# Local attention and a feed-forward net on one core: the first batch's values loaded once, by channels, and the instruction order written anew

## The chip, the core and the metric

The kernel runs on one core of a Trainium2 chip, in one launch. The metric is the device time of a launch in microseconds; with one core there is one time for each run.

## What is computed

For each of 4 batches and 8 heads, 768 queries of 64 channels attend to the keys within 15 positions of their own and, besides, to 24 block keys (the maximum of k over each block of 32 positions), whose values are the block means of v. The heads' results, side by side, are the 512 channels of 3072 tokens, which pass through a gated net of width 2048.

```python
k_sum = k.reshape(B, H, nb, block, D).max(axis=3)
v_sum = v.reshape(B, H, nb, block, D).mean(axis=3)
mask_l = np.abs(pos[:, None] - pos[None, :]) < window
scores_all = np.concatenate([np.where(mask_l, scale * q @ k.T, -1e9), scale * q @ k_sum.T + np.log(block)], axis=-1)
out = softmax(scores_all) @ np.concatenate([v, v_sum], axis=2)
x = out.transpose(0, 2, 1, 3).reshape(B * S, H * D)
h = x @ w_in
y = (h / (1 + np.exp(-h))) @ w_out
```

## The kernel before

The work is cut into 24 attention stages of 128 tokens (six of a batch) and 12 chunks of 256 tokens for the net. Stage s has scores (`scores`, L706), a softmax that DVE and ACT share (`job_a`: L731 subtracts and finds the maximum, L735 is the exponential), turned probabilities (L744 for the first four stages) and the product with the values (`job_c`, L776), after which `job_x` scales the result into the chunk's input. Chunk c and one eighth f of the net's width give a first product FFN1 (`job_f`, L997 in full float32 for the first chunk, L1005 with split float16 operands), a gate and a second product FFN2 (L1014). From the fifth chunk on, chunks go in pairs with seven products in place of eight (`pair_f`, L1082, L1133, L1204).

The sixteen weight tiles come as 64-bit words, 1 MB each, and are unpacked on chip: ACT (L913), POOL or DVE (L909, L911) and DVE (L915), which takes 1.2 us for each. Until its weight comes, the home of a weight (`wr`, named `wt` in the rows) holds data of the first batch: `staging` hands such homes out, and the load of that weight waits until the data in them has been read.

Values of the first batch come twice. `job_mean` loads them by tokens (`v0`, six tiles of 128 x 512, L624); TensorE multiplies each by a matrix `blocks` with 1/32 in the right places and so sums the block means in one bank (L628), DVE takes each tile's largest magnitude (L631). The means are copied from the bank five times (L265 on ACT, L269 on DVE): to the value tiles of stages 0 and 1, and to `vms`, from which `side_v` sends them to the value tiles of stages 2 and 3 by DMA. Those value tiles' other 96 rows, tokens of the two half stages, come from `v` by `main_v` (L603). The maximum over the six columns goes through a small matmul (`v_scale`, L513), whose result scales the first batch's values.

What engine does what, and in which order, is in no loop. Every step is a `plan.op` with the engines that can do it and what it reads and writes. The table `ORDER` (three characters a step) lists all steps in order with an engine for each, and `replay` takes it as it is when its length fits. Each engine runs its own list in that order, waiting where a step's inputs are not there. `replay` also fills holes that it foresees on PE at the start with matmuls on the identity (L386). SP issues nearly all DMAs, in order: a load whose destination is still in use holds back those behind it.

Of the kernel before, what the change touches and what calls it, by code (L numbers as in the profile page):

```python
# [9 lines left out]
F32 = mybir.dt.float32  # L10
# [5 lines left out]
ALU = mybir.AluOpType  # L16
# [242 lines left out]
def local_attn_ffn(ctx: ExitStack, tc: tile.TileContext, q0, qkT, qF, qkD, kF, v0, v, vR, w, out):  # L259
# [56 lines left out]
    blocks = const.tile([P, HWIN + 11 * 4], F32, name="blocks")  # L316
# [44 lines left out]
    vm_t = const.tile([P, 4, NB], F32, name="vm")  # L361
# [206 lines left out]
    def job_qk(s, prio):  # L568
        prio += nudge("qk", s)
        b, t = divmod(s, NTILE)  # L570
        if s < NPL:
            qk = qk_t[s % 2].bitcast(F32)[:, :4 * P].rearrange("p (a n) -> p a n", a=4)
            for hp in range(0, 4, 2):
                first = s == 0 and hp == 0
                plan.op({"dma": 545}, lambda e, hp=hp, first=first: (nc.scalar if first else nc.sync).dma_start(out=qk[:, hp:hp + 2], in_=q0[t, :, hp:hp + 2]), w=[("qk", s % 2, hp + i) for i in range(2)], prio=prio + hp // 2, cols=1 if first else 0)
            return
# [37 lines left out]
    def job_mean(prio):  # L614
        prio += nudge("mean")
        k = sbank()
        for t in range(NTILE):
            at = (NTILE - 1 - t) * 4
            if t < NPL:
                main_v(t, prio + 5)  # L620
            stg, key = staging(-1)
            src, cost = stg[:, :DM], 603
            parts = [(src, blocks[:, at:at + NKEY])]
            plan.op({"dma": 755}, lambda e, src=src, t=t: nc.sync.dma_start(out=src, in_=v0[t]), w=key, prio=prio)  # L624

# [12 lines left out]
        v_scale(0, prio)  # L638
# [252 lines left out]
    def job_w(fp, kind, prio):  # L891
# [7 lines left out]
        if wide:  # L899
            rt = home.rearrange("p (c i) -> p c i", i=2)  # L900
            low, top = rt[:, :, 0], rt[:, :, 1]
            sides = [k + x for k in mine for x in ((0,), (1,), (0, "side"), (1, "side"))]
# [515 lines left out]
NUDGE = {}  # L1418


_INS = ["q0", "qkT", "qF", "qkD", "kF", "v0", "v", "vR", "w"]


def _layout(inputs):
# [55 lines left out]
```

## Time and profile before

| | |
|---|---|
| median of 3 runs | 571.44 us (570.43 to 573.02) |
| profiled execution | 569.17 us, span 567.2 us |
| PE, DVE, ACT, POOL busy | 556.8, 467.8, 404.8, 210.8 us |
| DMA | 79.88 MB, 141 GB/s over the span |
| first float32 FFN1 matmul | 26.3 us after the span's start |
| last PE matmul ends | 563.1 us after the span's start |

Engines: PE is TensorE's matmul, DVE VectorE, ACT ScalarE, POOL GpSimd, SP the engine that issues DMAs. A busy PE is not PE at its peak, since matmuls overlap and their ends are modelled. Times within the span count from its first instruction. The column of the granted clock reads 1.00 in every stretch of this run.

### The profile page before, as it was taken

What the parts mean: (1) busy time and instruction counts of PE and PEld (TensorE: products, weight loads), DVE (VectorE), ACT (ScalarE), POOL (GpSimd) and SP (SyncE); (2) the same over time, 40 slices, a digit from 0 to 9 for tenths busy, and PEclk for the clock granted to TensorE, in tenths of its full rate; (3) what the DMA queues carried; (4) which work ended last, traced back from release to release, by engine and by line L of the source; (5) the groups of instructions that cost most, each with busy time, mean ns of one, the idle gap of its engine ahead of it and who ended that gap; (6) DMA issues with size and microseconds to landing.
All of it is one profiled execution on the core that took longest, in us unless ns stands there. A gap on an engine that the chain in (4) does not pass through costs nothing.

```text
span 567.2 us, 15166 instructions
## 1 busy us (share of the span) xinstructions
PE 556.8 (98%) x5811; PEld 392.0 (69%) x5811; DVE 467.8 (82%) x1245; ACT 404.8 (71%) x977; POOL 210.8 (37%) x261
## 2 busy tenths in 40 slices
PE   9899999999999999999999999999999999999997
PEld 5677666667676767767766656676666766688886
DVE  6898899999899888888687867866566698899996
ACT  4799999978878986766586866765755586477531
POOL 2052533253333641234724250346642453143310
PEclk9999999999999999999999999999999999999999
DMA  9969955486667672373525594454363212100002
GB/s 327 340 237 362 397 193 159 112 204 171 166 122 154 203 164 69 103 189 91 174 47 142 154 212 129 122 153 83 128 148 81 64 40 47 67 1 2 1 1 74
DMA packets 65351, 79.88 MB, mean 141 GB/s; under 512 B 46304, under 2 KB 48352, under 8 KB 63232
## 3 DMA queue, kind: packets, MB, share of 16 engines
q1 hardware_dynamic: 65136, 78.80, 49.0%
q8 instruction: 45, 0.74, 0.6%
q14 instruction: 26, 0.21, 0.2%
q10 hardware_dynamic: 144, 0.13, 0.1%
HBM read 59.97 MB, written 6.29 MB: 117 GB/s over the span
## 4 chain that ended last, share of the span: by engine, by line
PE 85%; DVE 6%; DMA 3%; ACT 3%; issue 1%; POOL 1%; SPq 1%; DVEq 0%; ACTq 0%; POOLq 0%
PE bank L1133 19%; PE bank L1082 19%; PE bank L1014 16%; PE bank L1005 13%; PE bank L1204 6%; PE bank L706 3%; PE bank L794 3%; PE bank L997 3%; DVE wt L1173 1%; PE bank L386 1%; DMA raw<-in_qkD_dram 1%; DVE t L1157 1%; DMA raw<-in_qF_dram 1%; DMA raw<-in_kF_dram 1%; ACT e L735 1%
## 5 line engine op out<-in xcount | busy, mean ns | idle before, releaser
L1082 PE MATMUL bank<-wt 128*128 128x256 f16 x1248 | 152.7, 273 | 1.5 <-DVE t L1062 0.9
L1082 PEld LDWEIGHTS <-wt 128*128 128x128 f16 x1248 | 121.1, 98 | 31.7 <-issue 2.6
L1014 PE MATMUL bank<-wt,g 128*128 128x512 f16 (+1 forms) x352 | 97.3, 420 | 0.0
L735 ACT ACTIVATE e<-e,mx 128x120 f32<-128x120 f32 x192 | 73.4, 384 | 19.9 <-DVE mx L731 19.7
L1005 PE MATMUL bank<-xh,wt 128*128 128x256 f16 x448 | 80.8, 273 | 0.0
L1005 PEld LDWEIGHTS <-wt 128*128 128x128 f16 x672 | 65.0, 98 | 16.1 <-issue 3.4
L1133 PE MATMUL bank<-wt,g 128*128 128x512 f16 x288 | 69.9, 380 | 0.1
L1005 PE MATMUL bank<-xl,wt 128*128 128x256 f16 x224 | 61.1, 273 | 0.0
L1061 ACT ACTIVATE t<-bank,asc 128x512 f32<-128x512 f32 x48 | 32.2, 682 | 27.0 <-PE bank L1082 23.8
L1014 PEld LDWEIGHTS <-g 128*128 128x128 f16 x288 | 27.9, 98 | 27.9 <-ACT t L1022 0.2
L1133 PE MATMUL bank<-wt,xl 128*128 128x512 f16 x192 | 46.1, 380 | 0.0
L731 DVE CUSTOM_DVE_ANT_0 e<-bank,masks,qsc 128x120 f32<-128x120 f32 x144 | 42.7, 337 | 3.9 <-PE bank L706 2.1
L1133 PEld LDWEIGHTS <-g 128*128 128x128 f16 x288 | 27.7, 98 | 25.2 <-POOL g L283 0.6
L1062 DVE SCALAR_TENSOR_TENSOR t<-t,bank 128x512 f32<-128x512 f32 x48 | 32.4, 684 | 14.0 <-ACT t L1061 13.5
L275 POOL TENSOR_SCALAR e<-e,sum 128x120 f32<-128x120 f32 x49 | 21.1, 437 | 53.9 <-DVE sum L750 49.8
L735 ACT ACTIVATION_READ_ACCUMULATOR e<-e,mx 128x1 f32 x192 | 36.1, 188 | 0.0
L283 POOL TENSOR_TENSOR g<-t,g 128x512 f16<-128x512 f32 x21 | 24.3, 1157 | 30.6 <-PE bank L794 7.4
L1133 PEld LDWEIGHTS <-xl 128*128 128x128 f16 x192 | 18.7, 98 | 17.5
L1022 ACT ACTIVATE t<-bank,asc 128x512 f32<-128x512 f32 x28 | 19.1, 683 | 13.3 <-PE bank L1005 13.2
L283 POOL TENSOR_TENSOR p<-e,p 128x480 f16<-128x480 f32 x19 | 20.8, 1096 | 20.6 <-ACT p L265 8.2
L265 ACT CAST g<-t 128x512 f16<-128x512 f32 x41 | 25.1, 612 | 4.2 <-DVE t L1024 2.3
L1108 DVE TENSOR_TENSOR bank<-bank,xh 128x256 f32<-128x256 f32 x32 | 13.8, 430 | 14.9 <-PE bank L1082 10.9
(266 smaller groups left out, 1187.3 us busy)
## 6 DMA issues: line engine op xcount, KB each, us to landing
wt<-in_w_dram SPq DMA_DIRECT2D x16, 1024.0 KB
raw<-in_qkD_dram SPq DMA_DIRECT2D x18, 624.0 KB
raw<-in_v_dram SPq DMA_DIRECT2D x20, 512.0 KB
out_dram<-raw SPq DMA_DIRECT2D x20, 256.0 KB
raw<-in_kF_dram SPq DMA_DIRECT2D x12, 384.0 KB
raw<-in_qF_dram SPq DMA_DIRECT2D x9, 512.0 KB
raw<-in_vR_dram SPq DMA_DIRECT2D x12, 384.0 KB
raw<-vms SPq DMA_DIRECT2D x40, 48.0 KB
```

The source lines that it names most:

```text
L265: nc.scalar.copy(out=out, in_=in_)
L275: nc.gpsimd.tensor_scalar(out=out, in0=in_, scalar1=by, scalar2=0.0, op0=ALU.mult, op1=ALU.add)
L283: eng[e].tensor_tensor(out=out, in0=in0, in1=in1, op=ALU.subtract)
L731: plan.op({"dve": 195 if b == 0 else 255}, lambda e, k=k, at=at, et=et, mx=mx: nc.vector.tensor_tensor_reduce(out=et, in0=bank[k][:, at:at ...
L735: plan.op({"act": 375}, lambda e, et=et, mx=mx, total=total: nc.scalar.activation(out=et, in_=et, func=AF.Exp, scale=-1.0, bias=mx, accum_ ...
L1005: nc.tensor.matmul(out=h[:, d * CH:(d + 1) * CH], lhsT=wt[f, 0][:, part, d, ct * P:(ct + 1) * P], rhs=x[:, ct, :], start=(ct == 0 and q == ...
L1014: nc.tensor.matmul(out=bank[to][:, :z0 - a0], lhsT=a[:, d * CH + u * P:d * CH + u * P + P], rhs=b[:, d, a0:z0], start=(opens and d == 0 an ...
L1061: plan.op({"act": 586}, lambda e: nc.scalar.activation(out=t, in_=h, func=AF.Tanh, scale=asc_t[c // 3 % 2][:, f:f + 1]), r=[("bank", k), ( ...
L1062: plan.op({"dve": 605}, lambda e: nc.vector.scalar_tensor_tensor(out=t, in0=t, scalar=1.0, in1=h, op0=ALU.add, op1=ALU.mult), r=[("bank", ...
L1082: nc.tensor.matmul(out=to, lhsT=w2[part][:, ct * P:(ct + 1) * P], rhs=xs[j][:, x, ct, :], start=(opens and ct == 0 and q == 0), stop=(ct = ...
L1133: nc.tensor.matmul(out=bank[to], lhsT=a[:, d * CH + v * P:d * CH + v * P + P], rhs=wt[f, 1][:, b][:, d, :], start=(opens and d == 0 and q ...
L1204: nc.tensor.matmul(out=place(m), lhsT=a[pa], rhs=b[pb], start=(opens and not right and q == 0), stop=(closes and q == 2), skip_group_check ...
```

## The change

The first batch's values now come by channels (`vR`, four tiles of 128 x 768, as the later batches' do). DVE sums each over blocks of 32 (L628 of the new kernel) and takes its largest magnitude (L630). TensorE turns the value rows of stages 0 and 1 out of these tiles (four groups of four transposes, L643, into banks 6 and 7) and the block sums (four transposes, L651, into bank 1, after GpSimd has put zeros ahead of the sums so that they land in rows 96 to 119). ACT and DVE copy them home, four copies of 96 rows and five of 24 rows, each of these with the factor 1/32 and all with the channels put back in order. `v0`, `blocks` and the six matmuls are gone, and so are two of the four loads of `main_v`. The queries of stages 1 to 3 come in one load each instead of two. `ORDER` is a new table for the whole kernel. In all, 35 filling matmuls become 62, and the other instructions of PE are the same in number save those named.

```diff
-    nc.vector.memset(blocks, 0.0)
-    for j in range(4):
-        nc.vector.memset(blocks[j * BLK:(j + 1) * BLK, HWIN + 20 + j:HWIN + 21 + j], 1.0 / BLK)
...
-    vm_t = const.tile([P, 4, NB], F32, name="vm")
+    vmp_t = const.tile([P, 4, NKEY], F32, name="vm")
+    vm_t = vmp_t[:, :, HWIN:]
+    nc.gpsimd.memset(vmp_t[:, :, :HWIN], 0.0)
...
-            for hp in range(0, 4, 2):
+            step = 4 if s else 2
+            for hp in range(0, 4, step):
...
     def main_v(t, prio):
         stg, key = staging(0)
         plain_v[t] = stg[:, :2 * DM].rearrange("p (a c) -> p a c", a=2), [key[0], key[0] + ("side",), key[0] + ("side", 1)]
-        plan.op({"dma": 1700}, lambda e: nc.sync.dma_start(out=plain_v[t][0][:HWIN], in_=v[0, t, :HWIN]), w=key, prio=prio)
+        if t < 2:
+            plain_v[t][1].insert(1, key[0] + ("u", 1))
+            return
+        plan.op({"dma": 1850}, lambda e: nc.sync.dma_start(out=plain_v[t][0][:HWIN], in_=v[0, t, :HWIN]), w=key, prio=prio)
...
     def job_mean(prio):
         prio += nudge("mean")
-        k = sbank()
-        for t in range(NTILE):
-            at = (NTILE - 1 - t) * 4
-            if t < NPL:
-                main_v(t, prio + 5)
+        for t in range(NPL):
+            main_v(t, prio + 5)
+        vrs, vkeys = [], []
+        for j in range(4):
             stg, key = staging(-1)
-            src, cost = stg[:, :DM], 603
-            parts = [(src, blocks[:, at:at + NKEY])]
-            plan.op({"dma": 755}, lambda e, src=src, t=t: nc.sync.dma_start(out=src, in_=v0[t]), w=key, prio=prio)
-
-            def mean(e, parts=parts, t=t):
-                for n, (rows, of) in enumerate(parts):
-                    nc.tensor.matmul(out=bank[k][:NKEY], lhsT=of, rhs=rows, start=(t == 0 and n == 0), stop=(t == NTILE - 1))
-
-            plan.op({"pe": 970}, mean, r=key, w=[("bank", k)], prio=prio, cols=2048)
-            plan.op({"dve": cost}, lambda e, src=src, t=t: nc.vector.tensor_reduce(out=am_t[:src.shape[0], t:t + 1], in_=src, axis=AX.X, op=ALU.max, apply_absolute_value=True), r=key, w=[("am", t)], prio=prio, port=())
+            nc.vector.memset(stg[:, :HALO], 0.0)
+            vr = stg[:, HALO:HALO + S]
+            vrs.append(stg)
+            vkeys += key
+            plan.op({"dma": 1250}, lambda e, vr=vr, j=j: nc.sync.dma_start(out=vr, in_=vR[0, :, j, :]), w=key, prio=prio)
+            plan.op({"dve": 869}, lambda e, vr=vr, j=j: nc.vector.tensor_reduce(out=vm_t[:, j, :], in_=vr.rearrange("p (n k) -> p n k", k=BLK), axis=AX.X, op=ALU.add),
+                    r=key, w=[("vm", j)], prio=prio, port=())
+            plan.op({"dve": 869}, lambda e, vr=vr, j=j: nc.vector.tensor_reduce(out=am_t[:, j:j + 1], in_=vr, axis=AX.X, op=ALU.max, apply_absolute_value=True), r=key, w=[("am", j)], prio=prio, port=())
+        def order(t):
+            return t.rearrange("n (h r q) -> n r h q", h=H, r=4)
+
+        def turned(k, rows):
+            return bank[k][rows].rearrange("n (r h q) -> n r h q", r=4, h=H)
+
         for t in range(2):
             for u in range(2):
-                to, key = plain_v[t][0][HWIN:NKEY, u], plain_v[t][1][1 + u:2 + u]
-                plan.op({"act": 478, "dve": 598}, lambda e, k=k, to=to: copy(e, to, bank[k][HWIN:NKEY]), r=[("bank", k)], w=key, prio=prio, port=())
-        plan.op({"act": 478, "dve": 598}, lambda e, k=k: copy(e, vms_t[HWIN:NKEY], bank[k][HWIN:NKEY]), r=[("bank", k)], w=["vms"], prio=prio, port=())
-        am_sum(NTILE, prio)
+                k, at = (6, 7)[u], t * P + u * HALF
+
+                def part(e, k=k, at=at):
+                    for j in range(4):
+                        nc.tensor.transpose(out=bank[k][:HWIN, j * P:(j + 1) * P], in_=vrs[j][:, at:at + HWIN], identity=ident)
+
+                to, key = plain_v[t][0][:HWIN, u], plain_v[t][1][u:u + 1]
+                plan.op({"pe": 520}, part, r=vkeys, w=[("bank", k)], prio=prio, cols=512)
+                plan.op({"act": 605, "dve": 605}, lambda e, k=k, to=to: copy(e, order(to), turned(k, slice(0, HWIN))), r=[("bank", k)], w=key, prio=prio, port=())
+
+        def turn_sums(e):
+            for j in range(4):
+                nc.tensor.transpose(out=bank[1][:NKEY, j * P:(j + 1) * P], in_=vmp_t[:, j, :], identity=ident)
+
+        plan.op({"pe": 520}, turn_sums, r=[("vm", j) for j in range(4)], w=[("bank", 1)], prio=prio, cols=512)
+        low = slice(HWIN, NKEY)
+        homes = [(plain_v[t][0][low, u], plain_v[t][1][2 + u:3 + u]) for t in range(2) for u in range(2)] + [(vms_t[low], ["vms"])]
+        for to, key in homes:
+            plan.op({"act": 605, "dve": 605}, lambda e, to=to: times(e, order(to), turned(1, low), 1.0 / BLK), r=[("bank", 1)], w=key, prio=prio, port=())
+        am_sum(4, prio)
         v_scale(0, prio)
...
-_INS = ["q0", "qkT", "qF", "qkD", "kF", "v0", "v", "vR", "w"]
+_INS = ["q0", "qkT", "qF", "qkD", "kF", "v", "vR", "w"]
```

The order moves at three places. DVE, from the copies of the turned values to the second half of `xp`, the input of the first FFN1; before (`bank_181` holds the block means, `bank_182` the stage's attention product, L915 is the weight's unpacking):

```order
L269 COPY vms<-bank_181 24x512
L269 COPY wt<-bank_181 24x512
L816 RECIPROCAL ss_150<-ss_150 128x8
L818 CAST sh_152<-ss_150 128x8
L269 COPY wt<-bank_179 120x512
L819 TENSOR_TENSOR sh_152<-ss_150,sh_152 128x8
L832 TENSOR_TENSOR xp<-bank_182,xr_154 128x4x128
L516 TENSOR_REDUCE sc_139<-bank_181 128x1
L517 TENSOR_SCALAR sc_139<-sc_139 128x1
L518 TENSOR_SCALAR sc_139<-sc_139 128x1
L915 SCALAR_TENSOR_TENSOR wt<-wt 128x1024
L832 TENSOR_TENSOR xp<-bank_182,xr_155 128x4x128
```

and after (`bank_176` and `bank_177` hold turned values or, for L853, the product; L936 is the unpacking):

```order
L269 COPY wt<-bank_174 120x512
L269 COPY wt<-bank_176 96x4x8x16
L836 TENSOR_SCALAR ss_145<-ss_145 128x8
L837 RECIPROCAL ss_145<-ss_145 128x8
L839 CAST sh_147<-ss_145 128x8
L840 TENSOR_TENSOR sh_147<-ss_145,sh_147 128x8
L853 TENSOR_TENSOR xp<-bank_177,xr_149 128x4x128
L936 SCALAR_TENSOR_TENSOR wt<-wt 128x1024
L346 COPY masks<-masks 128x120 x2
L347 MEMSET masks 64x15
L348 MEMSET masks 64x17
L853 TENSOR_TENSOR xp<-bank_177,xr_150 128x4x128
```

Two of the five small copies of means stood here before; now turned values and probabilities do, the maximum over the partition sums (L516 to L518) has gone behind, and the edges of the masks (L346 to L348) have come ahead.

DVE behind the second half of `xp`, after (before, four rows of L631 stood ahead of it instead, and behind it came L731, L911 and L915):

```order
L936 SCALAR_TENSOR_TENSOR wt<-wt 128x1024
L958 TENSOR_SCALAR wm<-wm 128x1
L630 TENSOR_REDUCE am<-wt 128x1 x2
L752 ISA e,mx<-bank_174,band 128x120
L752 ISA mx 128x1
L630 TENSOR_REDUCE am<-wt 128x1
L936 SCALAR_TENSOR_TENSOR wt<-wt 128x1024
L504 TENSOR_REDUCE am<-am 128x1
L1045 SCALAR_TENSOR_TENSOR g_167<-t_165,bank_170 128x512
L269 COPY wt<-bank_175 120x512
L836 TENSOR_SCALAR ss_144<-ss_144 128x8
L514 TENSOR_REDUCE sc_134<-bank_176 128x1
```

The four reductions for the largest magnitude (L630, one more at row 72, just behind `xp`) now stand between the softmax of stage 2 and the unpackings L936, ahead of the first gated product L1045.

SP's loads of the weights; before (`wt_64` and on are the homes of the weights, even numbers of the first product; `wt_68` to `wt_71` held `v0`):

```order
L903 DMA wt_64<-in_w_dram 128x2048
L603 DMA wt_76<-in_v_dram 96x1024
L575 DMA qk0_128<-in_q0_dram 128x256
L603 DMA wt_77<-in_v_dram 96x1024
L575 DMA qk0_128<-in_q0_dram 128x256
L903 DMA wt_66<-in_w_dram 128x2048
L903 DMA wt_65<-in_w_dram 128x2048
L903 DMA wt_68<-in_w_dram 128x2048
L903 DMA wt_70<-in_w_dram 128x2048
L575 DMA qk1_129<-in_q0_dram 128x256 x2
L903 DMA wt_67<-in_w_dram 128x2048
L603 DMA wt_76<-in_v_dram 96x1024
```

and after (`wt_68` to `wt_71` hold `vR`):

```order
L924 DMA wt_64<-in_w_dram 128x2048
L924 DMA wt_65<-in_w_dram 128x2048
L924 DMA wt_66<-in_w_dram 128x2048
L924 DMA wt_67<-in_w_dram 128x2048
L612 DMA wt_76<-vms_133 24x512 x2
L574 DMA qk1_123<-in_q0_dram 128x512
L924 DMA wt_70<-in_w_dram 128x2048
L605 DMA wt_76<-in_v_dram 96x1024
L924 DMA wt_68<-in_w_dram 128x2048
L924 DMA wt_69<-in_w_dram 128x2048
L671 DMA raw2_121<-in_v_dram 128x1024
L924 DMA wt_72<-in_w_dram 128x2048
```

The first four weights now follow each other, and the weights in `wt_70`, `wt_68`, `wt_69` (in this order) come behind the `vms` copies and the last queries.

## Rows read from the trace of the kernel before

**Rows 1.** The profile's page, part 1: busy time, share of the span, instructions of each engine.

```profile
PE 556.8 (98%) x5811; PEld 392.0 (69%) x5811; DVE 467.8 (82%) x1245; ACT 404.8 (71%) x977; POOL 210.8 (37%) x261
```

**Rows 2.** Waits of PE from 28 us on: line, whom it waited for: us in total, times, longest.

```profile
PE bank L1082 <- DVE t L1062: 0.9, 2, 0.8
PE bank L706 <- DVE wt L280: 0.5, 1, 0.5
PE bank L706 <- DVE qk L595: 0.5, 2, 0.3
```

**Rows 3.** The chain that ended last, 0 to 70 us, in order: start us, us, what.

```profile
7.20 1.05 PE bank L628 x2
...
9.45 0.44 PE bank L744 x4
...
25.14 0.92 issue
...
26.37 1.92 PE bank L997 x8
...
34.57 0.57 PE bank L826 x16
...
42.17 1.73 PE bank L997 x8
...
47.56 1.08 PE bank L776 x32
...
51.44 1.72 PE bank L1014 x4
```

**Rows 4.** Stretches: busy us of PE, PEld, DVE, ACT, POOL; clock, DMA share, GB/s.

```profile
5.00:10.00 5.00, 5.00 (x63) 3.51 (x65) 4.25 (x13) 1.70 (x9) 0.00 (x0) 1.00 1.05 389
14.00:20.00 6.00, 4.92 (x64) 2.72 (x64) 4.54 (x22) 4.77 (x19) 1.10 (x1) 1.00 1.04 245
20.00:33.00 13.00, 11.77 (x182) 10.29 (x183) 11.57 (x38) 10.61 (x27) 2.50 (x3) 1.00 1.02 405
```

**Rows 5.** Groups of DVE instructions, 0 to 30 us: count | busy us, mean ns | idle.

```profile
L731 DVE CUSTOM_DVE_ANT_0 e<-bank,band 128x120 f32<-128x120 f32 x23 | 5.3, 277 | 1.5 <-PE bank L706 1.5
L631 DVE TENSOR_REDUCE am<-wt 128x1 f32<-128x512 f32 x6 | 4.0, 682 | 0.0
L457 DVE TENSOR_REDUCE km<-wt 128x24 f32<-128x768 f32 x4 | 3.7, 950 | 1.7 <-DMA wt<-in_kF_dram 1.7
L915 DVE SCALAR_TENSOR_TENSOR wt<-wt 128x1024 uint32<-128x1024 uint32 x2 | 2.4, 1224 | 0.3 <-ACT wt L913 0.3
...
L516 DVE TENSOR_REDUCE sc<-bank 128x1 f32<-128x128 f32 x1 | 0.3, 281 | 0.0
...
L517 DVE TENSOR_SCALAR sc<-sc 128x1 f32<-128x1 f32 x1 | 0.2, 153 | 0.0
```

**Rows 6.** Timeline, 16 to 26 us: start us, us, engine, line, operation, shapes.

```profile
18.55 0.70 DVE L269 COPY vms<-bank 24x512 f32<-24x512 f32 x1 [0.43 <-ACT wt L265]
...
19.89 0.70 DVE L269 COPY wt<-bank 24x512 f32<-24x512 f32 x1 [0.64 <-ACT wt L265]
...
24.59 0.68 DVE L832 TENSOR_TENSOR xp<-bank,xr 128x512 f32<-128x512 f32 x1
```

**Rows 7.** The tile `vms` in the whole span: its rearranged copies, min/median/max ns.

```profile
L556 DVE TENSOR_SCALAR vms<-bank x3: 670/679/679, 131.8 to 370.4; 24x512 f32<-24x512 f32 x3
```

**Rows 8.** SP's timeline, 0 to 110 us: issue of four weight loads.

```profile
12.04 5.61 SPq L903 DMA_DIRECT2D wt<-in_w_dram  x4
```

**Rows 9.** Waits of the SP queue, 0 to 110 us.

```profile
SPq L903 <- PE bank L706: 14.2, 1, 14.2
```

**Rows 10.** Timeline, 0 to 16 us: the filling matmuls on the identity.

```profile
1.36 4.88 PE L386 MATMUL bank<-ident 128*128 128x256 bf16 x22 [1.36 <-POOL ident masks.py:199]
...
8.08 1.36 PE L386 MATMUL bank<-ident 128*128 128x256 bf16 x11
```

More of the change, by code (lines that the diff above doesn't have):

```diff
@@ L258, in local_attn_ffn @@
 @with_exitstack
-def local_attn_ffn(ctx: ExitStack, tc: tile.TileContext, q0, qkT, qF, qkD, kF, v0, v, vR, w, out):
+def local_attn_ffn(ctx: ExitStack, tc: tile.TileContext, q0, qkT, qF, qkD, kF, v, vR, w, out):
     nc = tc.nc
@@ L572, in job_qk @@
             qk = qk_t[s % 2].bitcast(F32)[:, :4 * P].rearrange("p (a n) -> p a n", a=4)
-            for hp in range(0, 4, 2):
+            step = 4 if s else 2
+            for hp in range(0, 4, step):
                 first = s == 0 and hp == 0
-                plan.op({"dma": 545}, lambda e, hp=hp, first=first: (nc.scalar if first else nc.sync).dma_start(out=qk[:, hp:hp + 2], in_=q0[t, :, hp:hp + 2]), w=[("qk", s % 2, hp + i) for i in range(2)], prio=prio + hp // 2, cols=1 if first else 0)
+                plan.op({"dma": 545 if step < 4 else 770}, lambda e, hp=hp, first=first: (nc.scalar if first else nc.sync).dma_start(out=qk[:, hp:hp + step], in_=q0[t, :, hp:hp + step]), w=[("qk", s % 2, hp + i) for i in range(step)], prio=prio + hp // 2, cols=1 if first else 0)
             return
@@ L901, in job_w @@
             low, top = rt[:, :, 0], rt[:, :, 1]
-            sides = [k + x for k in mine for x in ((0,), (1,), (0, "side"), (1, "side"))]
+            sides = [k + x for k in mine for x in ((0,), (1,), (0, "side"), (1, "side"), ("u", 1), ("side",), ("side", 1))]
             plan.op({"dma": 2750}, lambda e: nc.sync.dma_start(out=home, in_=src.bitcast(U32)), w=mine + sides + whole, prio=prio - TUNE["w_dma"] + nudge("wd", fp, kind))
@@ new lines @@
+    "0710cz0qf0dj07b0250r407l0sn0d507x0dt0d902z0850dp03e03w0dz0df03m09x0440a204q0a703t0b905i0ac05c04g0530c00fv0bg0e104x058046"
+    "0p90bq0bm04n0af0bw0kb0ca0c60e81ip09q0an04d0cg0p30ei0ci0en0es0ex0ar0cq0f00pc0eb0f80qm1ii0fz0fc0rh0pi03j1ae0rb0ie0vk0hk0gq"
+    "0gg01p0i40gm0g60hu1aj0gw0rk0gc0ik0hq0pm02p0t00rq1b802a0tc0qs0ia1ar0h00uv0341bd0i01j60h60qv0im05m1av0vx0r10h80it05p1ay0vr"
+    "0j305w0610j80660jd0ji0su0hf06b0jl06g06l0w00iw0jt1bl0t30pp0kk0tj0tp0pw1bp0fi1b30xs0m50q70ll0x30kr0q30jx0ay0v20mz1bx0mf0rw"
@@ new lines @@
+    "0ts0v71jb0k40mp0lb0rx0l10kx1cw0fm0ty0k70kg0l70s40b11c20n50sg0w50xz01u1280lh0y30zb1d10ml1000vb0lr1iw0mb0mv1pz0y80xa1c71ir"
+    "14g1qe0no0nt0wa0u20qb0n71cf0lt1d90ny0u51bs0o30uc0m10ne0uj1ji0s91cj0xg1dd0o60un0wd0nh0wk0xj0ye1cr13r0od0ww0vh0oi0yk0ur1cm"
+    "0oo12f0os12k1dl1jm0t90sj1pf1e011j0zi1p512o0zn1ez0wz1071e50zr0yl1f41ed0ys10d1dx1j30z31eh1dg1q51en10g14n1eu1fc0z71dt10m1fy"
+    "1fg14t1qk1fm1jp14w1qq1g313y0yx1pk1k610s1441my12t1ft1gb1n81qb1470zx1gx1r81kg0wr1gf15z1ne1jw1gm1mo10t11q1h21101kq12y11u0xp"
@@ new lines @@
+    "1gs11z1k21ha1ps1me1kc1ep1he1kw1251pv1tu1hk11c1re1qt1661p01hr16a1km11f1mk1521tz16f14d1311581uy1381mu1qz13k16l1591v31r515g"
+    "16p11516u13n1u71rx16x1fo1rk1741791l01vb17e1s717j17o1l515l1pc1rn17t1n41gn17y1vf19e1ll1lg1ub1lb1i419h1z41vl1uh1hm1ni13d1lq"
+    "1nn1ul19n1831o21sn1ns1o71ny1ut1vp1s419r1od1w21lv1oh1se1m121t1vx1oq1hy1ru15s1zl1zb24u1w71zv22d1ol21z20522n1a71si22315v1uo"
+    "1m81wf2291wj1sq19x25o1x61sx1m31t222t1t71tc2011th1vs1a122j1wp2511tm1xb1tr1wt25g22x1ab2561x11zh1zr25k1xj1ww25a20b3vf1xn26i"
@@ new lines @@
+    "2g220f1xt23220k20z25u33820q29j21520v1xx2g721a23m26021e24q1y523826x23d26o3yh21i23i23s3ym2aa1y01ym2gf23y26u2gj1yq2h61942cs"
+    "2gp2ep2c82ci2ce2d21ou2gv2ak2co1yc2cy2hb2aq2a01yg2d829q1972a62452h12hj2dc2402ag2dh2hn2dt29w2gw2ew3042f12hu2732632fb21n2ia"
+    "3vi2hx2dn1yx2au2if2az2f52dx2e22be2e72ff2i52in1z12ed2qx2b52ir2bk2l21892bb2ek2692je2bp2nr2ob2792bt2493vp26f2lj2ol2l92iy2jj"
+    "2m324h2902m92j32fj24l2or2c22i02lt2jr2o130b2o72jv2lz2j918d2k12r42lp27g2lf2yy18t27n27d2k52952r927q2md2z327x2rj2822872rd2bx"
@@ new lines @@
+    "2oh2j428c2zb28h2rn2nx2ef2kd2mi28m2ms29c2ov2p02pk2mz2zf2k82pc2n32mo29g2n830w2zl2ne2ku18j2kk2sa2ky2ph2p62zr2ko2pq3112tb2sh"
+    "2th2pu2zx28t2uz3192vj2sr2vp2v92t12xg2zs31d2t72q32sx2vt18n2vz32031j2nl2sn31n2v53252vf39a2fo2tl2w32tq2w839f31v18x32d2ng2wj"
+    "2u132h2u731q2we2py2wo30e32n2xm33b33y2y232r2ya3682fv36d32z2y62xs2fz3432xw35234b33i3if2tw34f2yf36k3bq34l2uc3572ug34p2rr2wt"
+    "30j2wy2uk34x35f36p3cr3bx3ch2x42q735j3im3ir35q3f93ef3ff37035t3cx2xb3j13c73ep33l3cd3612x63iv30p3j53753cn2rw3yr3ez3ev3f541h"
@@ L1418 @@
+    "9xm9xra6wa70a7x9tk9toa7ba7f9roa879vra17a3za1b9vu9wwa3ta1ga1la8h9vz9x0a8ra96a1qa1va91a759xv9xza9ga02a05a49a22a43a9ba7la7p"
+    "a26a2aa9qaahaama9vaaraawa4fab1a4gab5a58a5ca9laaaaa0abvabzaa5abla4labbabfabpa5ha5ra5va5ma0aa50a4qa6la6pa4va61a65a6ba6f")
 NUDGE = {}
-_INS = ["q0", "qkT", "qF", "qkD", "kF", "v0", "v", "vR", "w"]
+_INS = ["q0", "qkT", "qF", "qkD", "kF", "v", "vR", "w"]
 def _layout(inputs):
```

117 lines of the change are left out of this document (46 added, 71 removed).

## The prediction

> **What bounds the kernel now.** I read the page first: PE is busy for 556.8 of 567.2 us [rows 1]. So the time is PE's work plus the stretches in which PE has nothing of its own to do. I then asked for PE's waits behind the start: from 28 us on the three largest come to 0.9 + 0.5 + 0.5 = 1.9 us [rows 2]. What is left is the start, and there "busy" misleads: the filling matmuls count as busy, 22 of them in 4.88 us and 11 in 1.36 us [rows 10], though they compute nothing. The chain shows when useful work closes up: the first float32 FFN1 group stands at 26.37 us, right behind a pause of 0.92 us in which PE waited for nothing that the profile shows [rows 3]; behind it PE works without a break. A change at the start is worth what it moves that point, plus the PE work that it moves across it, plus the waits that it makes behind it.
>
> What releases FFN1 is DVE: the second half of its input `xp` starts at 24.59 and takes 0.68, so it is done at 25.27 [rows 6]. Ahead of it DVE is held up twice by the copies of the block means, which alternate with ACT on one bank: 0.43 us ahead of one copy and 0.64 ahead of the other [rows 6]. From 20 to 33 us DVE is busy for 11.57 of 13 us [rows 4]. DVE is therefore the engine on which this change is costed.
>
> **The change, part by part.** The sum is made against the profiled execution, 569.17 us, which lies 2.27 us below the median of 571.44; the same difference is then put on the median.
>
> *PE at the start.* Six block-sum matmuls of 1.05 us (a pair of passes each [rows 3]) go, 6.3 us. Twenty transposes come; four of the same size take 0.44 [rows 3], so 5 x 0.44 = 2.2. PE is relieved by 4.1 us, but ahead of FFN1, where it has holes: the new order puts 62 fillers in place of 35. At 1.36/11 = 0.124 us [rows 10] the 27 more are 3.3 us, so the table itself gives most of the relief back as filling. I take 0 for it. The cover is DVE's chain; if PE were the bound there after all, the end would be 4.1 us earlier, which is a rival below.
>
> *DMA at the start.* 1.57 MB of `v0` (6 x 128 x 512 x 4 bytes) are replaced by 1.57 MB of `vR`, and two loads of 96 x 1024 x 4 bytes (0.79 MB in all) are gone. In the stretch in which they moved the rate was 245 GB/s at a share of 1.04 instead of 405 GB/s [rows 4], so they were worth 0.79/0.245 = 3.2 us of a full DMA. The first weight no longer has to share with them. But FFN1 waits for `xp`, not for the weight, so I count 0. Three loads of queries fewer are on SP, not on the chain: 0. On these loads the stretch from 5 to 10 us, when the transfers were of 131 to 393 KB, shows 389 GB/s at a full share [rows 4]: transfers in flight together hide each other's latency. The Trainium skill, "DMA: Bandwidth & Descriptors", section on the anatomy of one DMA, gives about 2.0 us fixed for each DMA on the GpSimd path besides its bytes; taken for these and as a serial cost, three loads fewer would be an estimated 6 us. The trace disagrees at 389 GB/s, and I follow the trace.
>
> *DVE ahead of FFN1.* It loses six reductions of 0.682 [rows 5], 4.1 us, and gains four block sums; the keys' reduction of the same shape takes 0.950 [rows 5], so 3.8. It makes five copies from banks (three of values, two of sums) where it made two: 3 x 0.70 = 2.1 more [rows 6]. That the copies put channels back in order should not cost: a later batch's rearranged copy of this kind takes 0.679 at most [rows 7]. The maximum's three small steps (0.281 + 2 x 0.153 = 0.6 [rows 5]) move behind. Two steps on the masks, about half a microsecond each, trade places: 0. Together 3.8 - 4.1 + 2.1 - 0.6 = +1.2 us of work. Of waits the 0.43 + 0.64 = 1.07 ahead of the old copies go. A new one comes of the same kind: DVE's second copy of sums waits for two of ACT's on the same bank, 2 x 0.58 less the two softmax steps that DVE has meanwhile, 2 x 5.3/23 = 0.46 [rows 5], so 0.70. (0.58 is what ACT's copies must take between DVE's in rows 6: DVE's first ends at 19.25, and its second begins at 19.89 after 0.64 of waiting.) `xp` is then done at 25.27 + 1.2 - 1.07 + 0.70 = 26.1, and FFN1 starts right behind it, at 26.2, where it started at 26.3, since PE's pause of 0.92 now lies beside DVE's work: **-0.1**. Without the new wait, and with 0.3 more saved, it would be -1.2; with no old wait saved and the pause of 0.92 once more, +1.8.
>
> *The maximum's matmul.* It moves from a hole of PE to behind FFN1. It has a quarter of the columns of a block-sum matmul of 1.05 [rows 3], about 0.3: **+0.3**.
>
> *DVE behind FFN1.* The largest magnitudes were found before `xp`; now four reductions of about 0.95 stand behind it, among softmax steps and weight unpackings of 1.224 [rows 5]. DVE was busy there already, but the new list sends two maxima of weights to ACT. PE's list behind 26.2 is: FFN1 for two eighths, 4 x 1.73 to 1.92 [rows 3], say 7.3; two groups of transposes 0.9; the small matmul 0.3; then one FFN2 group at 34.7. DVE's list from 26.1 to the gated product that this FFN2 reads is 4 x 0.95 + 8 x 0.23 + 2 x 1.224 + 0.3 for small steps + 0.7 = 9.1, so 35.2: PE waits 0.5. Further on PE has FFN2 1.72, scaling 0.57, the attention product 1.08, the scores of stage 3 and two FFN2 groups [rows 3] before the third eighth; DVE has some 2.7 of copies and small steps, two unpackings, a gated product, five softmax steps, a product of 0.7 and the unpacking of that eighth's weight. By the same addition PE is there 0.7 us too early. I take **+0.7** for this part, the last wait alone, since 0.5 on an addition of 9.1 is less than it can tell; the ends are 0 (before, PE had no wait there) and 2.4 (twice the 0.5 + 0.7 that the addition finds).
>
> *The rest of the table.* All other lists are new, with the same PE work. Waits of 1.9 us [rows 2] can vanish or double; I take **0**, with ends of -1.9 and +1.9.
>
> The sum is -0.1 + 0.3 + 0.7 + 0 = +0.9 us: 570.1 for the profiled execution, and 572.3 against the median of 571.44. About 0.5%, 2.9 us, is what a measurement of this kernel tells from no change; the forecast is no change.
>
> **The rivals.** *The relief of PE comes through.* If the six matmuls of 1.05 us held up scores and turned probabilities at the start, all 4.1 us are gained, and the time is 567.3. For it: the block sums stand in the chain [rows 3]. Against it: 33 fillers run in the same stretch, and DVE, not PE, releases `xp`.
>
> *PE's clock falls.* The first 22 fillers took 0.222 us each, later ones 0.124 [rows 10]: PE starts at the lower of its levels, 1.2 GHz by the ratio, and goes to 2.4 GHz after some 4.9 us of work, while the granted clock's column reads 1.00 throughout. From 14 to 20 us PE was busy for 4.92 of 6 us [rows 4]; without the block sums that stretch thins out to copies, transposes and waits. If it fell there, the scaling, the attention products, the turned probabilities and the scores that lie between the copies and `xp` would take up to twice as long, 2 x 0.57 + 2 x 1.08 + 0.44 = 3.7 us more on the path: 572.3 + 3.7 = 576.0. Against it: the idle piece ahead of 20 us did no harm before, and fillers are planted there. The Trainium skill, "TensorE: Matmul & The Clock Gate", Part 4 (PE-mode transpose), says that transposes do not count as activity for the clock as matmuls do, which speaks for this rival; no row here shows it.
>
> *SP's queue is held up.* The four weights of the second and third place were issued from 12.04 on [rows 8]. Now the load into `wt_70` waits for the largest magnitude of the values that lie there, so till 27 us, and that into `wt_68` for the next two, till 32; behind them stands the value load of stage 2. At 405 GB/s a weight takes 2.6 us. The third eighth's weight is then there at about 37, unpacked by 40, and wanted at 43.5; the margin is some 4 us. SP lived with a hold of 14.2 us before [rows 9], which speaks against it. If DVE is later by 4 us and the slow value load (245 GB/s) stands ahead, PE waits 3 us more: 575.3, slower.
>
> **How the numbers follow.** Forecast 0.60, relief 0.20, clock 0.09, queue 0.11. The likeliest time is 572.3; its own range is 569.0 to 575.0. With the rivals, 567.0 to 575.8 leaves out less than 2 in 10. Faster by over 0.5% (under 568.6) is the relief: 0.20. Slower by over 0.5% (over 574.3) are the clock, the queue, and no more: 0.20. The rest, 0.60, is no change.
>
> **What would show it.** In the profile after, the chain's first FFN1 group should stand between 25 and 28 us, with DVE's `xp` right ahead of it; PE's waits up to 45 us should name DVE and come to about 1 us; matmuls of the first chunk should keep their 1.73 us for each eight. An FFN1 ahead of 24 us, or PE's useful work 3 us ahead at the first split FFN1, would be the relief; groups of twice the length between 15 and 30 us the clock; a wait of PE or ACT on a weight's load the queue. Waits of over 4 us behind 60 us would show that the rest of the table, which I take as neutral, decided.

## The result, and the profile after

The changed kernel takes 564.93 us (median of five executions; four lie from 564.55 to 565.40, the fifth, of 1162.65 us, was disturbed and is in no comparison) against 571.44 (five, 570.39 to 573.02): a ratio of 0.9885, interval 0.986 to 0.9909. That is 6.5 us faster, below the range's low end of 567.0. The profiled execution took 564.81 us, with a span of 563.0 where it was 567.2. The page's part 1 of the changed kernel, answering [rows 1]:

```profile
PE 554.9 (99%) x5846; PEld 394.5 (70%) x5846; DVE 467.8 (83%) x1238; ACT 404.3 (72%) x983; POOL 221.2 (39%) x270
```

DVE's busy time is the same to 0.1 us, and PE's is 1.9 us less though 27 filling matmuls have come. The waits of PE in the whole span (line, whom it waited for: us in total, times, longest), answering [rows 2]:

```profile
PE bank L847 <- ACT wt L273: 1.4, 1, 1.4
PE bank L384 <- POOL ident masks.py:199: 1.4, 1, 1.4
PE bank L765 <- ACT e L756: 0.5, 2, 0.2
PE bank L847 <- DVE sh L839: 0.2, 1, 0.2
```

All four stand ahead of FFN1. The three of [rows 2], 1.9 us behind 200 us, have gone, and the pause of [rows 3] too. The chain that ended last, from 20 to 36 us, answers [rows 3]:

```profile
21.03 0.39 ACT e L756 x2
...
21.89 0.18 DVE sh L839
...
22.11 0.78 PE bank L847 x16
...
23.01 1.15 PE bank L797 x32
24.16 1.25 PE bank L727 x64
25.41 7.11 PE bank L1018 x32
...
33.39 0.22 PE bank L511 x2
33.62 1.72 PE bank L1035 x4
```

The 64 score matmuls of stage 2 run through without a pause, and FFN1 follows (its first matmul starts at 25.34, where it was 26.30). All 32 matmuls of four groups follow each other in 7.11 us; turned probabilities, the small matmul of the maximum (L511) and the first FFN2 (L1035) come behind them without a wait.

The stretch from the start of FFN1 to the end of PE's last matmul, before and after (from and to in us, length, then busy us and count of PE, PEld, DVE, ACT, POOL; granted clock, DMA share, GB/s):

```profile
26.30:563.15 536.85, 534.18 (x5463) 376.45 (x5458) 447.66 (x1160) 389.72 (x932) 206.22 (x242) 1.00 0.48 132
25.34:558.86 533.52, 533.15 (x5467) 376.87 (x5460) 446.47 (x1155) 388.74 (x939) 215.60 (x251) 1.00 0.49 131
```

The account of the profiled executions, from the two traces: FFN1 starts 0.96 us earlier; PE's idle time from FFN1 to its last matmul goes from 2.67 us (536.85 less 534.18 busy) to 0.37 (533.52 less 533.15), 2.3 less; the work in that stretch is 1.03 less; the tail is 0.09 longer. Together -4.2, the difference of the spans. The other 2.2 us of the medians' 6.5 lie in the choice of the execution: that of before was profiled at 569.17, 2.3 under its median, that of after at its median.

### The profile page after: what moved, and what is told of

It reads as the page before. It is cut to its first block, busy times and chain, and to the rows that moved or that the text cites. A ratio compares the mean times of both kernels' runs of the same rounds, so it can differ in the third digit from the quotient of the medians.

```text
span 563.0 us, 15215 instructions
## 1 busy us (share of the span) xinstructions
PE 554.9 (99%) x5846; PEld 394.5 (70%) x5846; DVE 467.8 (83%) x1238; ACT 404.3 (72%) x983; POOL 221.2 (39%) x270
## 4 chain that ended last, share of the span: by engine, by line
PE 88%; DVE 6%; ACT 2%; issue 1%; DMA 1%; SPq 0%; POOL 0%; DVEq 0%; POOLq 0%; ACTq 0%
PE bank L1103 23%; PE bank L1154 22%; PE bank L1035 15%; PE bank L1026 12%; PE bank L1225 6%; PE bank L727 3%; PE bank L815 3%; PE bank L1018 3%; DVE wt L1194 1%; DMA wt<-in_kF_dram 1%; ACT wt L273 1%; DVE t L1178 1%; ACT e L756 1%; PE bank L797 1%; DVE vm L628 0%
## 5 line engine op out<-in xcount | busy, mean ns | idle before, releaser
L1035 PE MATMUL bank<-wt,g 128*128 128x512 f16 (+1 forms) x352 | 96.9, 419 | 0.1
L1035 PEld LDWEIGHTS <-g 128*128 128x128 f16 x288 | 27.8, 98 | 28.2 <-POOL g L283 0.6
L283 POOL TENSOR_TENSOR g<-t,g 128x512 f16<-128x512 f32 x27 | 31.3, 1159 | 34.6 <-DVE qsc L489 9.6
L275 POOL TENSOR_SCALAR e<-e,sum 128x120 f32<-128x120 f32 x53 | 24.4, 468 | 49.2 <-DVE sum L771 34.0
L273 ACT ACTIVATE e<-e,sum 128x120 f32<-128x120 f32 x75 | 26.1, 386 | 4.4 <-DVE sum L771 4.4
L283 POOL TENSOR_TENSOR p<-e,p 128x480 f16<-128x480 f32 x20 | 22.2, 1111 | 17.3 <-ACT p L265 8.6
```

The costliest lines, as they stand in the source:

```text
L273: nc.scalar.activation(out=out, in_=in_, func=AF.Copy, scale=by)
L283: eng[e].tensor_tensor(out=out, in0=in0, in1=in1, op=ALU.subtract)
L1035: nc.tensor.matmul(out=bank[to][:, :z0 - a0], lhsT=a[:, d * CH + u * P:d * CH + u * P + P], rhs=b[:, d, a0:z0], start=(opens and d == 0 an ...
```

## The experiments

Theory **table**: the gain is waits behind 180 us that the new order does not have. Theory **start**: it is made ahead of FFN1, by the values. Theory **supply**: what the start gains is only the pause of 0.92 us, in which PE waits for its instructions. Times are medians, beside runs of the kernel before on the same chip. In kernels with an edit above the steps, lines are 1 to 5 higher.

**The kernel before, unchanged** (before_again).

> The kernel before once more, for a second profile. If the spread of its times (570.4 to 573.0, where the profiled execution took 569.2) comes from waits that differ from execution to execution, this profile shows other waits of PE than the first one's 0.92 (pause in the scores of stage 2) and 1.9 us (behind 200 us), and its span stands apart from 567.2 by just that. If the waits are the same to 0.1 us and the time is not, the spread lies outside of the span.

570.06 us (ten executions, 567.52 to 572.80; the 29 of before beside it 568.83 to 573.47). The profiled one took 572.8, and its waits of PE from 28 us on are not those of [rows 2]:

```profile
PE bank L794 <- DMA tt<-p: 1.4, 1, 1.4
PE bank L1082 <- DVE t L1062: 1.3, 2, 1.1
PE bank L706 <- DVE wt L280: 1.0, 1, 1.0
PE bank L1014 <- ACT g L265: 0.5, 1, 0.5
PE bank L706 <- DVE qk L595: 0.3, 1, 0.3
PE bank L1133 <- POOL g L283: 0.3, 1, 0.3
```

4.8 us, where the same list of the first profile comes to 2.3, with 1.9 in its three largest. The two spans lie 3.6 us apart: FFN1 is 0.2 later (26.51), PE's idle time behind it 2.8 longer, and its work there 0.6 more. So between these two executions most of the difference is such waits. One profile shows one draw from them, and the first was a good one.

**Fewer filling matmuls in the kernel before** (before_22fill, before_31fill).

```diff
-            for _ in range(fills):
+            for _ in range(min(fills, 22 - fed)):
                 self.fill()
+                fed += 1
```

> The kernel before without the 13 filling matmuls that follow the first 22. Theory supply (the pause of 0.92 us in the scores of stage 2 is PE waiting for its next block of instructions): 26 instructions fewer ahead move the place of the pause in the program by 26 instructions, so it falls elsewhere or vanishes, FFN1 at 25.4 to 25.6, the time up to 0.9 us less. If the pause is a wait for data that the profile does not show, it stays at the same instruction, FFN1 at 26.3. If PE's clock falls without the filling, groups between 8 and 25 us take up to twice as long and FFN1 comes after 27.

566.69 us (566.00 to 567.13), ratio 0.9924, interval 0.9898 to 0.995: 13 filling matmuls, taken out of a start where nothing waited for them, give back 4 us, where up to 0.9 was expected. The start of the timeline tells a part of it: the pause is gone and FFN1 starts at 25.41, behind 0.32 us that PE's timeline also puts down to "issue":

```profile
24.63 0.68 DVE L833 TENSOR_TENSOR xp<-bank,xr 128x512 f32<-128x512 f32 x1
25.41 1.97 PE L998 MATMUL bank<-xp,wt 128*128 128x256 f32 x8 [0.32 <-issue]
```

`xp` is done at 25.31, and FFN1 follows 0.10 later, so here DVE does release it. In the kernel before, `xp` was done 1.03 us ahead of FFN1. PE's waits from 28 us on:

```profile
PE bank L707 <- DVE wt L281: 0.8, 1, 0.8
PE bank L707 <- DVE qk L596: 0.3, 1, 0.3
PE bank L1083 <- DVE t L1063: 0.2, 1, 0.2
```

Matmul by matmul against the first profile of before, this kernel is 0.9 us ahead at FFN1, stays so until 330 us, and gains 2 us more between 330 and 363 us, where the other waited.

> The kernel before with 4 filling matmuls fewer (31 of 35). Theory supply: the pause stands after a fixed number of PE's instructions, since a block of them is late; it stood behind 58 of the 64 score matmuls of stage 2 and moves by 4 pairs, to behind 62 of the 64; it ends 2.4 to 2.6 us after the transfer of 16 KB of instructions starts, FFN1 at 26.1 to 26.4. If it waited for data, it stays behind 58 of the 64.

One execution, 571.72 us. The last scores of stage 2 on PE's timeline, and the transfer of instructions in the stretch from 23.4 to 23.5 us (queue: packets, MB, share):

```profile
24.54 0.26 PE L707 MATMUL bank<-km,qk 64*64 64x24 f32 x6
25.98 0.29 PE L707 MATMUL bank<-km,qk 64*64 64x24 f32 x2 [1.18 <-issue]
26.20 1.13 PE L998 MATMUL bank<-xp,wt 128*128 128x256 f32 x4
```

```profile
q8 instruction: 1, 0.02, 67.2%
```

Two are left where six were: the pause has moved by exactly the 4 pairs that are missing ahead of it. It ends 2.56 us after a transfer of 16 KB of instructions starts (23.42; in the kernel before 23.59 and 26.06, so 2.47; in before_again 23.69 and 26.28). Supply holds: a wait for data would have stayed at its instruction. That PE ran through the short score matmuls faster than the next block of its program came is inferred from the place and the time; the trace does not name the engine that a transfer of instructions is for.

**PE late by work in place of a pause** (before_22fill_late, after_late).

The edit of after_late; before_22fill_late has the same eight, behind the 22 of above.

```diff
+            if late and self.ops[i][1].__name__ == "bare_go":
+                late = False
+                for _ in range(8):
+                    self.fill()
             self.ops[i][1](e)
```

> The kernel before with the first 22 filling matmuls, and 8 more right ahead of the first FFN1: PE is about 1 us later there, by work and not by a pause (8 x 0.124 us), and the blocks of instructions end 10 instructions earlier than in the kernel before. Theory phase (the waits of PE behind 180 us come back when PE is 1 us later than the loads and the other engines): 570 to 571, with a spread of 4 us. Theory supply alone (blocks of instructions that end elsewhere took the waits away): 566.7 + 1.0 = 567.7, with a spread of about 1 us.

569.69 us (568.91 to 570.50), ratio 0.9987, interval 0.9967 to 1.0007: nearly all of the 4 us is lost again, though FFN1 is only 0.74 us later than with 22 fillers (26.15). PE's waits from 28 us on are 2.7 us instead of 1.3, and its last matmul ends 2.93 later (563.19 against 560.26). So theory phase is nearer: in the old order, being late at FFN1 costs several times what it is. A side result bears supply out once more:

```profile
24.91 0.94 PE L391 MATMUL bank<-ident 128*128 128x256 bf16 x7
26.03 0.28 PE L391 MATMUL bank<-ident 128*128 128x256 bf16 x1 [0.18 <-issue]
```

With 13 fillers fewer ahead, what is left of the pause stands 13 pairs further on: behind the six remaining scores and seven of the new fillers.

> The changed kernel with 8 more filling matmuls right ahead of the first FFN1: the partner of the kernel before with 22 + 8. PE is 0.9 to 1.0 us later there. Theory late start (the new order has slack): 565.8, spread under 1.5 us. If any order pays several times for a late FFN1: 568 to 569.

566.33 us (565.76 to 566.89), ratio 0.9911, interval 0.9882 to 0.994. FFN1 is 0.81 later (26.15), and the median 1.4: less than half of what the old order makes of it. Its only wait of PE from 28 us on is 0.2. In the profile PE's last matmul ends 0.7 later than in the changed kernel, about one to one; the rest is a longer tail behind that matmul (4.7 against 4.1). The same stretch as above, with the eight fillers ahead of FFN1 in the old order and in the new one:

```profile
26.15:563.19 537.04, 534.17 (x5459) 376.61 (x5458) 447.39 (x1154) 389.29 (x932) 206.53 (x242) 1.00 0.47 132
26.15:559.58 533.43, 532.98 (x5462) 376.92 (x5460) 445.94 (x1152) 388.45 (x937) 213.62 (x250) 1.00 0.48 131
```

PE is idle for 2.87 us of the one and for 0.45 of the other.

**The changed kernel without its 40 extra fillers** (after_22fill; the edit of before_22fill).

> The changed kernel with the first 22 filling matmuls alone, 40 fewer. Theory supply (PE pauses in a burst of short matmuls when the next 16 KB block of its instructions is still on the way; the changed kernel is spared since its blocks end elsewhere): 80 instructions fewer put the end of a block into the scores of stage 2, so a pause of about 1 us stands there, FFN1 starts at 26.2 to 26.5 instead of 25.3, and the time is 1 to 3 us more than the 564.9 of the changed kernel. Theory clock (the fillers keep PE's clock up): groups of PE between 10 and 25 us take up to twice as long, FFN1 after 27. If the fillers do neither, FFN1 stays at 25.3 and the time at 564.9.

565.77 us (564.86 to 565.94), ratio 0.9911, interval 0.9878 to 0.9944. Supply foretold FFN1 and is wrong on the cause: there is no pause, and the time is 0.8 us more, not 1 to 3. Theory clock has the cause, though FFN1 does not come after 27. Stretches of this kernel, then of the changed one (busy us of PE, PEld, DVE, ACT, POOL; granted clock, DMA share, GB/s):

```profile
5.00:10.00 5.00, 2.07 (x42) 1.67 (x39) 4.82 (x17) 1.62 (x8) 1.36 (x6) 0.82 0.97 358
10.00:14.00 4.00, 3.75 (x70) 2.91 (x69) 2.85 (x14) 2.58 (x11) 0.00 (x0) 0.50 0.83 301
14.00:18.00 4.00, 4.00 (x46) 3.54 (x44) 3.84 (x13) 2.78 (x9) 0.00 (x0) 0.50 0.94 340
```

```profile
5.00:10.00 5.00, 4.67 (x62) 3.56 (x60) 4.80 (x16) 1.62 (x8) 1.36 (x6) 1.00 0.98 367
10.00:14.00 4.00, 4.00 (x89) 3.54 (x88) 4.00 (x20) 3.07 (x13) 0.00 (x0) 1.00 1.01 353
```

Behind a stretch in which PE was busy for 2.07 of 5 us, the granted clock is 0.50 (1.2 GHz) from 10 to 18 us, and the eight turned values of that time take 1.9 us instead of 1.0. FFN1 starts at 26.44. The fillers of the changed kernel avert what I had as the clock's rival; they are worth 1.1 us at FFN1 and 0.8 us by the medians, with executions that overlap.

**Halves of the two tables.** The steps of one table up to some 80 or 100 us, then the rest in the other's order, on the engines of the other's table; 22fill as above.

> The changed kernel, with its own table for the first 381 steps (some 80 us) and then the order and the engines of the table before. Theory table (most of the gain is waits that the new order takes away behind 200 us): PE's waits behind 200 us are back at about 2 us, the time is 568 to 570. Theory start (the gain is made in the first 80 us, by the values that come by channels): 565 to 566. Theory supply (what the start gains is only the pause of 0.92 us): FFN1 stays at 25.3, and the time is 0.9 us under the kernel before.

> The kernel before, with its own table for the first 392 steps (some 80 us) and then the order and the engines of the new table. Theory table: PE's waits behind 200 us fall to some 0.3 us, the time is 566 to 568. Theory start: 570 to 572. Theory supply: FFN1 at 26.3 with the pause of 0.92 us as before.

> The changed kernel with its own table for the first 493 steps (some 100 us), then the old order and engines: a second seam, 20 us later. FFN1 starts at 25.3 without a pause. Theory late start (the old order has no slack behind 180 us, and what FFN1 is late costs four times: the 0.9 us pause made 3 to 4 us in the kernel before): with FFN1 early the old order gives 566 to 567.5, as the kernel before did without its pause. Theory new order (the old order is bad by itself): 570 or more.

> The kernel before with its own table for the first 490 steps (some 100 us), then the new order and engines. The pause is there again, FFN1 at 26.2 to 26.5. Theory late start: the new order has slack and passes the pause on one to one, 566 to 567. If the new order too makes three or four of it: 569 to 571.

> As the run before it, with the first 22 filling matmuls alone, so without the pause: FFN1 at 25.4. Theory late start: 565 to 566, 0.9 us under its partner; values by channels are then worth nothing by themselves, since the old values with the new order come to the time of the changed kernel, 564.9, within 1 us.

| start (FFN1) | rest | cut at | us | ratio, interval |
|---|---|---|---|---|
| new (25.3) | old | 80 | 572.42 | 1.0031, 1.0012 to 1.0051 |
| old, pause (26.0) | new | 80 | 572.48 | 1.0027, 1.0014 to 1.004 |
| new (25.3) | old | 100 | 569.53 | 0.9982, 0.9963 to 1.0001 |
| old, pause (26.3) | new | 100 | 568.42 | 0.9955, 0.9938 to 0.9971 |
| old, 22 fillers (25.3) | new | 100 | 566.72 | 0.9932, 0.9907 to 0.9956 |

None of the five times lies in a range that its expectation gives. In oldstart_newrest the cut at 80 us makes a wait at the seam, which ends at 87.9 us; the whole list of its waits from 60 us on is

```profile
PE bank L1014 <- ACT g L273: 4.3, 1, 4.3
PE bank L706 <- ACT wt L273: 0.2, 1, 0.2
```

and without the 4.3 it would stand at an estimated 568.2, where the cut at 100 us puts it. In newstart_oldrest it is not the seam itself: 1.1 us of PE's waits lie at 90 and 104 us, and 6.2 behind 150 us. At 100 us, the expectation of 566 to 567.5 for the new start with the old rest missed: PE waits there for 3.4 us behind 130 us. So an early FFN1 alone doesn't settle the old order. That a seam disturbs it as a pause does would explain this and is not shown. With the new rest the pause costs 1.7 us by the medians (568.42, from 567.29 to 569.78, against 566.72, from 566.21 to 569.51), with the old one 4. This seam too makes waits: between 100 and 130 us PE waits for 2.0 us in the profile with the pause and for 2.8 in the one without, so the 1.7 is uncertain by as much.

**Both kernels by the planner** (ORDER emptied).

> The kernel before with an empty table, so that its own planner sets the order: the partner of the run after it. A planned order is worse than a table that was searched for, so 575 to 590; what matters is the difference of the two.

> The changed kernel with an empty table, so that the same planner sets the order. Theory values (values by channels are worth something by themselves, 4.1 us of PE at the start): 3 to 5 us under its partner. Theory table (they are worth nothing at the start, since DVE's additions take their place, and the new table made the gain): within 2 us of its partner, FFN1 within 1 us of the partner's.

634.39 (629.89 to 635.88) and 636.20 us (635.63 to 640.20). Both lie far above the 575 to 590 expected. The times are within 2 us, but FFN1 starts at 49.0 and 35.8, so the planner's start is 13 us shorter with the values by channels; one wait of 8.4 us on DVE, which ends at 129 us, and others behind it stand against that. These orders are too far from the tables to say what the values are worth in them; the pair is inconclusive.

**The copies from one bank, grouped** (after_grouped). In ORDER, DVE makes its two copies of sums behind its four maxima, so that ACT's three come one after the other, and ACT's last exponential of stage 1 goes ahead of the copy of stage 0's product; 7 fillers more are planted. DVE's list, then ACT's:

```diff
-L277 TENSOR_SCALAR wt<-bank_171 24x4x8x16
 L752 ISA e,mx<-bank_173,band 128x120
 L752 ISA e,mx<-bank_172,band 128x120
-L277 TENSOR_SCALAR wt<-bank_171 24x4x8x16
 L752 ISA e,mx<-bank_172,band 128x120
+L752 ISA e,mx<-bank_173,band 128x120
+L277 TENSOR_SCALAR wt<-bank_171 24x4x8x16 x2
 L269 COPY wt<-bank_177 96x4x8x16
-L752 ISA e,mx<-bank_173,band 128x120
...
-L756 ACTIVATE e,ss_145<-e,mx 128x120 x3
+L756 ACTIVATE e,ss_145<-e,mx 128x120 x4
 L265 COPY xr_149<-bank_171 128x512
-L756 ACTIVATE e,ss_145<-e,mx 128x120
```

> The changed kernel with the copies of the block sums grouped: ACT makes its three one after the other, then the four exponentials of stage 1; DVE makes the four maxima of stage 1 first and its two copies behind. In the changed kernel ACT waited 0.88 and 0.76 us for DVE's copies from the same bank, and the exponentials ended at 21.4. Theory start (these alternating copies hold FFN1 in both kernels; 1.07 us of such waits I took to go with the change): the exponentials end by 20.2, FFN1 starts at 24.3 to 24.7 and the time is 0.6 to 1.0 us under the changed kernel's, 564.0 to 564.4. If the maxima or the weight's unpacking take over, FFN1 stays within 0.3 us of 25.3 and the time at 564.9.

564.04 us (563.41 to 565.16), ratio 0.9888, interval 0.9829 to 0.9947 (beside six runs of before only). ACT in the changed kernel, and then here:

```profile
17.21 0.59 ACT L273 ACTIVATE wt<-bank 24x512 f32<-24x512 f32 x1 [0.88 <-DVE wt L277]
18.56 0.59 ACT L273 ACTIVATE wt<-bank 24x512 f32<-24x512 f32 x1 [0.76 <-DVE wt L277]
```

```profile
16.25 1.06 ACT L273 ACTIVATE wt<-bank 24x512 f32<-24x512 f32 x2
```

The exponentials end at 19.0 instead of 21.4, FFN1 starts at 24.40 instead of 25.34, and the span is 562.3 instead of 563.0. The median is 0.9 us under the changed kernel's, with executions that overlap: the gain at the start is shown, that at the end is likely. It is the fastest of all kernels here. That two engines took turns on one bank is in the program, where each waits for the other's copy. It is the bank that they share: in the kernel before, DVE's copy to `vms` waited for a copy of ACT's to another tile [rows 6]. The Trainium skill, "PSUM — Partial Sum Buffer", section "PSUM bank collisions raise a hardware error", says that two engines must not access the same quadrant of a bank at once, reads among themselves included. The trace agrees as far as it goes: none of these copies overlap, and no run here lets them.

## Why the prediction was wrong

- **PE at the start, taken at 0 of 4.1 us: right.** Without the pause, FFN1 starts at 25.41 with the old values (before_22fill) and at 25.34 with the new ones. The relief of PE went into fillers, which the clock needs. The rival "relief" gave a time of 567.3, the nearest of the four, for a reason that the runs refute: that its number is near is luck.
- **FFN1, -0.1: measured -0.96, inside its ends.** The size failed, and the engine. I let `xp` on DVE set the start, at 26.1. It is done at 25.14 (24.45 and 0.69): from 5 us to its end DVE has 1.5 us more work (17.34 before, 18.84 after), where I had 1.2, and 1.6 less idle time (2.93 before, 1.30 after), where I had 0.37. FFN1 starts 0.2 behind it, when the scores are through. The waits of the new kind fell on ACT, 0.88 and 0.76, not 0.70 on DVE, and went on over the exponentials to stage 1's product; after_grouped shows it. And the pause, which I named and then set beside DVE's work, was no part of the data's flow: it was the instruction supply. Against the old start without it (25.41) FFN1 moved by 0.07, so 0.9 of the 0.96 is the pause. In the changed kernel transfers of 16 KB of instructions start at 19.87 and 25.14, not at 23.6, and no pause stands in the scores; that the ends of the blocks fall outside of them there, with another count of instructions ahead, is inferred.
- **The maximum's matmul, +0.3: measured 0.22**, in the chain.
- **DVE behind FFN1, +0.7: measured 0**, my lower end. The gated product starts at 32.52 where I had 34.5. One us of this is the earlier start; the rest is that I added durations, to 8.4 us from the end of `xp` on, where the list takes 7.4. Instructions of DVE that follow each other overlap by some 0.08 us in the trace (a reduction of 0.94 at 25.06, the next at 25.92), which over the 16 of this list is 1 us.
- **The rest of the table, 0 with ends of 1.9: this is the step that failed**, and with it the rule ahead of the sum, by which a move of FFN1 and the waits behind it are counted apart. The term is worth 2.3 us of waits and 1.0 of work in the profiled pair, and some 2 more against other executions of before. I read 1.9 us of waits as the size of the matter, from one execution; before_again has 4.8. And the waits hang on FFN1: the kernel before pays about 4 us for 0.9 there, which no single profile shows, while the new order passes a late FFN1 on about one to one. So about 4 of the 6.5 us can be had in the kernel before without the change, by leaving out 13 fillers. None of the signs that I had named stood for such a gain: for the table I had named only waits that come.

  The 1.0 of work is not the new order's own. The kernel before with 22 fillers, then before_again, from FFN1 to PE's last matmul:

```profile
25.41:560.26 534.85, 533.47 (x5458) 376.81 (x5458) 448.05 (x1162) 390.51 (x934) 205.39 (x243) 1.00 0.47 133
26.51:566.76 540.25, 534.82 (x5464) 376.64 (x5458) 448.18 (x1160) 389.37 (x931) 205.33 (x242) 1.00 0.47 130
```

In the same old order PE's busy time is 533.47, 534.18 and 534.82 us where its idle time is 1.4, 2.7 and 5.4: most of the difference comes and goes with the waits. No run was made on the reason.
- **The queue's rival** did not reach PE, which waits for no weight. The sign that I had named, a wait of PE or ACT on a weight's load, is there once before 60 us, at 47.5 on ACT, and costs PE nothing:

```profile
ACT wt L934 <- DMA wt<-in_w_dram: 0.4, 1, 0.4
```

What stays open: which wait tips the old order, since DVE, ACT, POOL and a turned tile's DMA each release PE late in one profile or another; and how much of the 6.5 us the values by channels would carry with a table of their own for the old start. The nearest pair, old values without the pause and with the new rest (566.72) against the changed kernel (564.93), holds them to 1.8 us, seam included. The seam's own waits, 2.8 us in the profile of the slowest execution (569.51), are more than that, so these runs do not tell what the values are worth from nothing.

## What to carry to other kernels

Where a hand-made order leaves the bounding engine no slack, a profile is one draw: take two before you call its waits the size of what a new order can gain, and test it by making the engine a microsecond late. An "issue" pause in a burst of short instructions is worth one run with a few instructions fewer ahead of it. Add up starts of consecutive instructions, not durations, and ask of every bank that two engines read which of them is made to wait.

## What the runs showed of the hardware

- PE paused for 0.8 to 1.2 us in a burst of 64 short matmuls at a place fixed by the count of its instructions, until 2.4 to 2.6 us after a 16 KB transfer of instructions had started, while the DMA engines were at a full share. Moving 4 pairs out from ahead of it moved it by 4 pairs.
- 2.07 us of work in 5 us (mean granted clock 0.82) was followed by 8 us at a granted clock of 0.50, 1.2 GHz, through stretches in which PE was busy for 3.75 and 4.00 of 4 us with transposes and short score matmuls.
